# Attention's AV product with the exponentials as the stationary operand and a column of ones beside v

## The chip, the cores and the metric

The kernel runs on one core of one Trainium2 chip. The time is the device time of one execution in microseconds (us); the figure of a kernel is the median of its timed executions. Before the change it was 445.83 us (3 executions, 445.46 to 446.05). An execution counts as slow when it lies over 1.5% above the fastest of its kernel.

Engines: PE is TensorE (matmuls), "PEld" its weight loads, ACT is ScalarE, DVE is VectorE, POOL is GpSimd, SP is SyncE, which here only issues DMAs.

## The reference, cut to what matters

```python
# attention: q, k, v are [8 batches, 8 heads, 576, 64]; bias_table is [32, 8]
scores = q @ k.T / sqrt(64) + bias[bucket(|i - j|)]     # bias depends on the distance only
attn   = softmax(scores)                                # over the 576 keys
x      = (attn @ v), heads side by side                 # [4608, 512]
# "MoE" block (one expert)
h   = x @ w_in                                          # 512 -> 2048
g   = h + sin(alpha * h)**2 / (alpha + 1e-9)
out = g @ w_out                                         # 2048 -> 512, [4608, 512] fp32
```

The kernel computes exp(score/8) without subtracting the maximum, multiplies it by exp(bias) (a mask that differs from a constant only near the diagonal), forms the product with v and the sum over the keys, and divides.

## The kernel before: the parts that matter

One batch is 576 rows; there are 8 batches and four pairs of heads in each. Scores are kept transposed: keys on the partitions, queries on the free axis. `u` is the tile of exponentials of one pair, `[128 keys, 9 key blocks, 576 queries]`, where block 8 holds the last 64 keys of both heads.

A small scheduler in the kernel, run when the kernel is built, puts all work into a fixed order per engine, from estimated durations. Output matmuls (`mo`) are "fillers": they have no urgent reader, so the scheduler drops them into PE's waits during the attention of the next batch.

```python
def mm2(out, lhsT, rhs, start, stop):          # a 128-wide matmul as two of 64 stationary columns
    for z in range(2):
        nc.tensor.matmul(out=out[64*z : 64*z+64], lhsT=lhsT[:, 64*z : 64*z+64], rhs=rhs, ...)

# QK: one unit = one PSUM bank of scores = one exponential of 384 columns
for g in range(2):
    nc.tensor.matmul(out=sc.v[64*g : 64*g+64, ...], lhsT=kz[:, p, k0 : k0+64], rhs=qT[:, p, q0 : q0+n], ...)
nc.scalar.activation(out=u.v[:, k0 : k0+nc_, q0 : q0+n], in_=sc.v[...], func=AF.Exp, scale=0.125)

# AV: v is stationary, the exponentials stream through. y = 0: ones in place of v, so that the sums
# arrive on all 64 partitions of each head; y = 1: v itself. Columns streamed: 2 x 5 x n
for y in range(2):
    mm2(o[:, 0:n], vh if y else ones2, u.v[:, 8, q0 : q0+n], True, False)
    for c in range(4):
        for z in range(2):
            nc.tensor.matmul(out=o[64*z : 64*z+64, 0:n], lhsT=vs[..] if y else ones,
                             rhs=u.v[:, 4*z + c, q0 : q0+n], start=False, stop=(c == 3))
# 1/sum as exp(-ln(sum)) on ACT, then the product with it on DVE
nc.scalar.activation(out=ln.v[:, 0:n], in_=avs[0].v[:, 0:n], func=AF.Ln)
nc.scalar.activation(out=rd.v[:, 0:n], in_=ln.v[:, 0:n], func=AF.Exp, scale=-1.0)
nc.vector.tensor_tensor(out=xT[...], in0=avs[1].v[...], in1=rd.v[...], op=ALU.mult)

# ... cut: per batch, a table load, 16 sine units (PE sc -> ACT sine -> square -> DVE g), a table load
# ... cut: start-up: POOL reverses the mask table (m2, mh) that DMA brought in ascending order
```

The softmax here doesn't subtract the row's maximum and nothing guards it: scores larger than these inputs give would overflow.

Of the kernel before, what the change touches and what calls it, by code (L numbers as in the profile page):

```python
# [10 lines left out]
F16 = mybir.dt.float16  # L11
# [23 lines left out]
NBUF = {"sc": 4, "av": 2, "mo": 2, "u": 2, "g": 2, "s16": 3, "sq": 3, "outs": 2, "ln": 2, "rd": 2}  # L35


class Task:
    def __init__(self, engs, emit, deps, pri, nb=0.0):
        self.engs, self.emit, self.deps, self.pri, self.nb = engs, emit, list(deps), pri, nb  # L40
        self.allocs = []
        self.s_only = self.fill = self.tiled = False
        self.end = self.eng = None
# [11 lines left out]
class Plan:  # L55


    def __init__(self):
        self.tasks = []
        self.sin = self.in_qk = self.tiled = False  # L60
        self.used = self.share = 0
        self.warm = None
        self.rings = {k: [] for k in NBUF}

# [9 lines left out]
    def ready(self, t):  # L74
# [4 lines left out]
        for d in t.deps:  # L79
            if d.end is None:  # L80
                return None
            r = max(r, d.end - (LAT["PE"] if d.eng == "PE" and "PE" in t.engs else 0.0))
        for b in t.allocs:
            ring, n = self.rings[b.tag], NBUF[b.tag]
            if len(ring) >= n:
                for x in ring[-n].users:
                    if x.end is None:
                        return None
                    r = max(r, x.end)
        return r  # L90

    def run(self, t0):
        free = {e: t0 for e in ("PE", "ACT", "DVE", "POOL")}
        todo = list(self.tasks)
        while todo:
# [3 lines left out]
            for t in todo:  # L99
# [6 lines left out]
                for e in t.engs:  # L106
# [3 lines left out]
                    if e == "PE" and t.tiled != self.tiled:  # L110
                        st += D_MODE
# [29 lines left out]
            if e == "PE":  # L141
                self.tiled = t.tiled
# [9 lines left out]
            todo.remove(t)  # L152


WINDOW = 700
D_MODE = 0.0
WARM_END = 40.0
# [3 lines left out]
T_START = 5.4  # L161
T_M2 = 11.0
T_V0 = 13.0
T_TR1 = 34.0
T_W = 28.0
T_WO = 52.0
# [3 lines left out]
LN_PRI = -2000  # L170
# [17 lines left out]
def kernel(  # L188
# [49 lines left out]
    vs = [sgl.tile([128, 4, H, D], F16, name=f"v{i}") for i in range(2)]  # L238

    vhs = [sgl.tile([128, NP, 2, D], F16, name=f"vh{i}") for i in range(2)]  # L240
    ones = sgl.tile([128, D], F16, name="ones")
    ones2 = sgl.tile([128, 2, D], F16, name="ones2")
    m2 = sgl.tile([128, H, XW], F16, name="m2")
    mh = sgl.tile([128, NP, 192], F16, name="mh")
# [8 lines left out]
    m2r = wv[:, 2 * 5 * H * D : 2 * 5 * H * D + H * XW].rearrange("p (h x) -> p h x", h=H)  # L253
# [34 lines left out]
    def new_ln():  # L288
        return tp.tile([128, 384], F32, name="lnd", tag="lnd", bufs=NBUF["ln"])

    def new_rd():
        return tp.tile([128, 384], F32, name="rd", tag="rd", bufs=NBUF["rd"])

# [9 lines left out]
    def new_sc():  # L303
        return ps.tile([128, 512], F32, name="sc", tag="sc", bufs=NBUF["sc"])
# [14 lines left out]
    def load_kqT(t):  # L319
# [3 lines left out]
        nc.sync.dma_start(out=kz[64:128, :, S : 2 * S], in_=kraw[64:128, :, :])  # L323
        nc.sync.dma_start_transpose(out=qTs[t % 2][:, :, :], in_=staged_q.ap()[t])

    def load_v16(t):
        vp = v[t].rearrange("h s d -> s h d")
        for c in range(4):
            nc.gpsimd.dma_start(  # L329
                out=vs[t % 2][:, c], in_=vp[128 * c : 128 * c + 128],  # L330
            )
        vq = v[t].rearrange("(hp two) s d -> two s hp d", two=2)
        for z in range(2):
            nc.gpsimd.dma_start(
                out=vhs[t % 2][64 * z : 64 * z + 64, :, z, :], in_=vq[z, 512:S]
# [10 lines left out]
    def cast_v(eng, t):  # L346
        for c in range(4):
            eng.tensor_copy(out=vs[t][:, c], in_=vst[:, c])
        for z in range(2):
            eng.tensor_copy(  # L350
                out=vhs[t][64 * z : 64 * z + 64, :, z, :], in_=vhst[64 * z : 64 * z + 64]
# [18 lines left out]
    def clear_v(eng, i):  # L370
        eng.memset(vhs[i][0:64, :, 1, :], 0.0)
        eng.memset(vhs[i][64:128, :, 0, :], 0.0)

    def mm2(out, lhsT, rhs, start, stop):

        for z in range(2):
            nc.tensor.matmul(  # L377
                out=out[64 * z : 64 * z + 64], lhsT=lhsT[:, 64 * z : 64 * z + 64], rhs=rhs,
                start=start, stop=stop,
            )  # L380

    def warm(n):
        x = new_mo()
        for _ in range(n):
            mm2(x, zz[:, 0:128], zz, True, True)
# [6 lines left out]
    def load_m2r(h0, h1):  # L392

        nc.gpsimd.dma_start(
# [4 lines left out]
    def turn(p):  # L399
        nc.gpsimd.tensor_copy(  # L400
            out=m2[:, 2 * p : 2 * p + 2, :], in_=m2r[:, 2 * p : 2 * p + 2, ::-1]
        )

    load_nat(nat0[:, 0], 0, 2, k[0], nc.sync)
    nc.sync.dma_start(out=tabN, in_=bias_table)
    nc.sync.dma_start(out=phi_sb, in_=phi_h.ap())
    nc.sync.dma_start(out=id_sb, in_=idm.ap())
    load_nat(nat0[:, 1], 0, 2, q[0], nc.scalar)
# [4 lines left out]
    )  # L413
    nc.scalar.preload_act_table_set(EXP_SET)
    load_v32(0, nc.sync)
    for kq, src in ((0, k), (1, q)):
        load_nat(nat1[:, kq, 0:2], 2, 4, src[0], nc.gpsimd)

    nc.vector.memset(zz, 0.0)
    nc.vector.memset(kzs[0][0:64, :, S : 2 * S], 0.0)  # L420
    nc.vector.memset(kzs[0][64:128, :, 0:S], 0.0)
    clear_v(nc.vector, 0)
# [7 lines left out]
    nc.scalar.dma_start(out=e_dram.ap(), in_=e_sb)  # L430
    cast0(0, nc.vector)
    cast0(1, nc.gpsimd)
    nc.sync.dma_start(out=alphaN, in_=moe_alpha.rearrange("(f p) -> f p", p=128))
    nc.sync.dma_start(out=idf_sb, in_=idf.ap())
    nc.gpsimd.memset(ones, 1.0)
    nc.gpsimd.memset(ones2, 0.0)
    nc.gpsimd.memset(ones2[0:64, 0, :], 1.0)
    nc.gpsimd.memset(ones2[64:128, 1, :], 1.0)
    load_m2r(0, 2)
    for kq, src in ((0, k), (1, q)):  # L440
        load_nat(nat1[:, kq, 2:6], 4, H, src[0], nc.gpsimd)
    load_m2r(2, H)
    turn(0)
    cast_v(nc.gpsimd, 0)
    load_w_in16()
    for p in range(1, NP):
        turn(p)
    me = m2.rearrange("p (hp two) x -> p two hp x", two=2)
    nc.gpsimd.tensor_copy(out=mh[0:64, :, :], in_=me[0:64, 0, :, 0:192])
    nc.gpsimd.tensor_copy(out=mh[64:128, :, :], in_=me[64:128, 1, :, 64:256])  # L450
# [3 lines left out]
    clear_v(nc.gpsimd, 1)  # L454
    nc.gpsimd.memset(kzs[1][0:64, :, S : 2 * S], 0.0)
    nc.gpsimd.memset(kzs[1][64:128, :, 0:S], 0.0)
    cast_v(nc.gpsimd, 1)
# [14 lines left out]
    def plan_tr(t, p, kq, pri, nb, deps=()):  # L472
# [36 lines left out]
        return [plan.add(eng, cp, [m], pri, use=[b])]  # L509
# [18 lines left out]
    def plan_pair(t, p, kqt, first, gate, ub, band_nb):  # L528
# [3 lines left out]
        units, head = [], []  # L532
        for w in range(2):
            units += [(w, 4, 0)]
            for c in range(0, 4, 1 + w):
                units += [(w, c, 0), (w, c, 1)]
        if t == 0 and p == 0:
            units = [units[x] for x in (1, 3, 0, 2, 4)] + units[5:]
        for i, (w, c, z) in enumerate(units):
            q0, n = WIN[w]  # L540
            nc_ = 1 if w == 0 or c == 4 else 2
            b, sc = Buf("sc"), Cell()

            def qk(e, i=i, w=w, c=c, z=z, q0=q0, n=n, nc_=nc_, sc=sc):
# [8 lines left out]
                sc.v = new_sc()  # L553
                for y in range(nc_):
                    for g in range(2):
                        k0 = S * g + 512 if c == 4 else S * z + 128 * (c + y) + 64 * g
                        nc.tensor.matmul(  # L557
                            out=sc.v[64 * g : 64 * g + 64, n * y : n * y + n],
                            lhsT=kzs[t % 2][:, p, k0 : k0 + 64],
                            rhs=qTs[t % 2][:, p, q0 : q0 + n], start=True, stop=True,  # L560
                        )

            def ex(e, w=w, c=c, z=z, q0=q0, n=n, nc_=nc_, sc=sc):
                k0 = 8 if c == 4 else 4 * z + c
                nc.scalar.activation(  # L565
                    out=u.v[:, k0 : k0 + nc_, q0 : q0 + n], in_=sc.v[:, 0 : n * nc_],
                    func=AF.Exp, scale=0.125,
                )

            base = PB + 100 * (16 * p + i)  # L570
            m = plan.add({"PE": nc_ * t_pe(n)}, qk, kqt, base, after=head, new=[b] + ([ub] if i == 0 else []))
            head = head or [m]
            x = plan.add({"ACT": t_act(n * nc_)}, ex, [m] + gate, base + 20, use=[b, ub])
            if c == 4:
                if w == 0:
                    done[(w, 4, 0)] = done[(w, 4, 1)] = x
                    continue
# [5 lines left out]
                x = plan.add({"DVE": 0.17}, bh, [x] + mh_tasks, base + 10, nb=band_nb, use=[ub])  # L583
                done[(w, 4, 0)] = done[(w, 4, 1)] = x
                continue
            for y in range(nc_):
                done[(w, c + y, z)] = x
            if z == 0:
                continue
            for cc in range(c, c + nc_):  # L590
# [4 lines left out]
                def bd(e, cc=cc, lo=lo, hi=hi):  # L595
# [7 lines left out]
                x = plan.add({"DVE": 0.07 + (hi - lo) / 960.0}, bd,  # L603
                             [done[(w, cc, 0)], done[(w, cc, 1)]], base + 10, nb=band_nb,
                             use=[ub])
                done[(w, cc, 0)] = done[(w, cc, 1)] = x
        return u, done

    av_last = []
# [222 lines left out]
```

## Time and profile before

| reading | value | view |
|---|---|---|
| time | 445.83 us | timed executions |
| busy: PE / ACT / DVE | 95 / 86 / 59% of the span | page, part 1 |
| period of steady batches | 45.87 us | sine table loads in the timeline |
| exponential phase: PE, ACT busy | 28.74, 28.15 of 28.77 us | windows |
| sine phase: PE, ACT busy | 16.86, 15.87 of 16.86 us | windows |

Busy times and the chain, from the page (busy us, share of the span, x instructions; then the chain of work that ended last, by engine):

```profile
PE 423.1 (95%) x4934; PEld 306.1 (69%) x4934; DVE 262.4 (59%) x554; ACT 382.9 (86%) x834; POOL 84.5 (19%) x95
...
PE 71%; ACT 16%; issue 3%; DVE 3%; DMA 3%; POOL 2%; ACTq 0%; DVEq 0%; POOLq 0%
```

PE's 95% is no proof that PE is the limit: matmuls overlap and their ends are modelled. What tells is how far apart they start. L377 in these lines is line 377 of the kernel, the helper `mm2`.

The timeline of ACT shows one table load for the sine and one for the exponential per batch; here two sine loads four batches apart (start us, duration us, what):

```profile
189.24 1.28 ACT L756 ACT_TABLE_LOAD   x1
...
372.71 1.28 ACT L756 ACT_TABLE_LOAD   x1
```

(372.71 - 189.24) / 4 gives the period, 45.87 us. The windows view splits it (window, length, then busy us of each engine with its instructions, granted clock of PE, DMA share, GB/s). The first is a sine phase, the second an exponential phase, the third the same four batches:

```profile
core 0: us, PE busy (x) PEld busy (x) DVE busy (x) ACT busy (x) POOL busy (x), PEclk, DMA share, GB/s
97.59:114.45 16.86, 16.86 (x164) 11.12 (x160) 13.59 (x24) 15.87 (x25) 9.24 (x8) 1.00 1.75 180
114.45:143.22 28.77, 28.74 (x392) 22.55 (x389) 15.45 (x40) 28.15 (x74) 0.00 (x0) 1.00 0.30 44
189.24:372.71 183.47, 181.61 (x2188) 134.63 (x2185) 115.43 (x253) 178.90 (x397) 23.26 (x22) 1.00 0.60 72
```

ACT is busy 178.90 of 183.47 us, 97.5%.

The groups that the change touches (line, engine, operation, out<-in, shapes, count | busy us, mean ns of one | idle before them and who ended it):

```profile
L631 PE MATMUL av<-u,ones 128*64 128x384 f16 x256 | 27.6, 332 | 0.0
L647 ACT ACTIVATE lnd<-av 128x384 f32<-128x384 f32 x32 | 17.8, 556 | 1.9 <-PE av L631 1.0
L651 ACT ACTIVATE rd<-lnd 128x384 f32<-128x384 f32 x32 | 16.7, 523 | 1.0
L598 DVE TENSOR_TENSOR u<-u,m 128x512 f16<-128x512 f16 x64 | 28.3, 442 | 31.2 <-ACT u L565 27.9 <-POOL m L400 3.2
L631 PEld LDWEIGHTS <-v 128*64 128x64 f16 x512 | 30.7, 112 | 3.9
```

The waits between 10 and 50 us, the first batch (who waited <- for whom: us in total, times, longest):

```profile
DVE u L581 <- POOL mh L450: 6.6, 1, 6.6
...
PE sc L557 <- DVE qT L470: 5.3, 2, 4.6
```

### The profile page before, as it was taken

Reading aid. Unit: us, or ns where it says so; the run is one execution under the profiler, and the core shown is the slowest. Engines: PE = TensorE matmul, PEld = TensorE weight load, DVE = VectorE, ACT = ScalarE, POOL = GpSimd, SP = SyncE. Lnnn points to the kernel's source line nnn. Section 1 sums busy time; section 2 is a strip of 40 time slices with the busy share of each in tenths; the row PEclk is TensorE's granted clock in tenths of the full one; section 3 lists DMA queues with packets and bytes.
Section 4 is the critical chain, followed back from the end, with each engine's and each line's share of the span. In section 5 each row is a group of like instructions: output and inputs, shape, how many; then the busy total and the mean of one; then the engine's idle time right before and its main releaser. Section 6 shows DMA issues by size and latency. Waiting matters only on the chain.

```text
span 444.2 us, 12031 instructions
## 1 busy us (share of the span) xinstructions
PE 423.1 (95%) x4934; PEld 306.1 (69%) x4934; DVE 262.4 (59%) x554; ACT 382.9 (86%) x834; POOL 84.5 (19%) x95
## 2 busy tenths in 40 slices
PE   5579999999999999999999999999999999999996
PEld 3356657876688668865886688657876787666663
DVE  4447695549654865576456755685568545927400
ACT  3459999999999999999999999999999999946511
POOL 3792931016000700080008000400000000000000
PEclk8659999999999999999999999999999999999999
DMA  9999999939900996199209960980000000011111
GB/s 193 181 206 144 163 163 147 194 81 181 110 25 26 106 146 143 42 147 168 39 27 98 156 140 1 160 104 25 27 26 0 27 26 25 2 49 47 49 72 71
DMA packets 136118, 41.51 MB, mean 93 GB/s; under 512 B 122520, under 2 KB 130768, under 8 KB 136064
## 3 DMA queue, kind: packets, MB, share of 16 engines
q0 software_dynamic: 89392, 17.67, 47.3%
q1 hardware_dynamic: 46400, 22.79, 23.4%
q8 instruction: 38, 0.62, 0.6%
q10 hardware_dynamic: 272, 0.30, 0.2%
q14 instruction: 16, 0.13, 0.1%
HBM read 37.56 MB, written 16.52 MB: 122 GB/s over the span
## 4 chain that ended last, share of the span: by engine, by line
PE 71%; ACT 16%; issue 3%; DVE 3%; DMA 3%; POOL 2%; ACTq 0%; DVEq 0%; POOLq 0%
PE mo L377 24%; PE sc L377 18%; PE sc L557 14%; PE av L631 12%; ACT s L694 6%; ACT u L565 4%; PE av L377 3%; ACT L756 2%; ACT sq L701 2%; DVE g L708 1%; DMA w_out<-e_dram 1%; DMA tabL<-in_bias_table_dram 1%; DVE kz L470 1%; ACT rd L651 1%; ACT lnd L647 1%
## 5 line engine op out<-in xcount | busy, mean ns | idle before, releaser
L565 ACT ACTIVATE u<-sc 128x384 f16<-128x384 f32 x448 | 175.3, 527 | 7.6 <-PE sc L557 7.4
L377 PE MATMUL mo<-w_out,g 128*64 128x512 f16 x1152 | 172.2, 379 | 0.0
L557 PE MATMUL sc<-qT,kz 128*64 128x192 f16 (+1 forms) x1152 | 134.8, 296 | 8.8 <-DVE qT L470 5.3
L377 PE MATMUL sc<-xT,w_in 128*64 128x512 f16 x1152 | 132.7, 379 | 1.3 <-DVE g L708 1.3
L598 DVE TENSOR_TENSOR u<-u,m 128x512 f16<-128x512 f16 (+1 forms) x192 | 73.5, 400 | 72.1 <-ACT u L565 68.6
L557 PEld LDWEIGHTS <-kz 128*64 128x64 f16 x1152 | 84.7, 112 | 42.8 <-issue 10.6
L708 DVE SCALAR_TENSOR_TENSOR g<-sq,inv_a,sc 128x512 f16<-128x512 f16 x144 | 102.0, 745 | 20.6 <-PE mo L377 10.7
L377 PEld LDWEIGHTS <-w_in 128*64 128x64 f16 x1152 | 80.3, 110 | 44.1 <-issue 2.8
L694 ACT ACTIVATE s<-sc,alphaT 128x512 f16<-128x512 f32 x144 | 92.5, 678 | 3.5 <-PE sc L377 2.5
L377 PEld LDWEIGHTS <-g 128*64 128x64 f16 x1152 | 79.1, 110 | 22.5
L329 POOL DMA_DIRECT2D v<-in_v_dram x24 | 22.3, 1065 | 176.3 <-PE av L631 176.3
L701 ACT ACTIVATE sq<-s 128x512 f16<-128x512 f16 x75 | 47.2, 629 | 2.3
L662 DVE TENSOR_TENSOR xT<-av,rd 128x384 f16<-128x384 f32 (+1 forms) x68 | 29.4, 437 | 32.9 <-ACT rd L651 24.8
L631 PE MATMUL av<-u,ones 128*64 128x192 f16 (+1 forms) x512 | 44.8, 291 | 0.0
L631 PE MATMUL av<-u,v 128*64 128x192 f16 (+1 forms) x512 | 44.7, 291 | 0.0
L703 DVE TENSOR_TENSOR sq<-s 128x512 f16<-128x512 f16 x69 | 28.9, 420 | 11.4 <-ACT s L694 11.1
L647 ACT ACTIVATE lnd<-av 128x384 f32<-128x384 f32 x64 | 28.9, 451 | 7.3 <-PE av L631 6.5
L468 ACT ACTIVATE outs<-mo 128x512 f32<-128x512 f32 x15 | 8.9, 595 | 29.3 <-PE mo L377 29.3
L631 PEld LDWEIGHTS <-ones 128*64 128x64 f16 x512 | 30.8, 112 | 5.0
L631 PEld LDWEIGHTS <-v 128*64 128x64 f16 x512 | 30.7, 112 | 3.9
L651 ACT ACTIVATE rd<-lnd 128x384 f32<-128x384 f32 x64 | 28.7, 449 | 1.4
L377 PE MATMUL av<-u,ones 128*64 128x192 f16 (+1 forms) x128 | 20.5, 291 | 2.7 <-DVE u L581 2.7
(59 smaller groups left out, 194.0 us busy)
## 6 DMA issues: line engine op xcount, KB each, us to landing
out_dram<-outs SPq DMA_DIRECT2D x36, 256.0 KB, 2.0
staged_k<-in_k_dram POOLq DMA_DIRECT2D x6, 576.0 KB, 13.6
staged_q<-in_q_dram POOLq DMA_DIRECT2D x6, 576.0 KB, 16.7
kz<-kraw SPq DMA_DIRECT2D x12, 288.0 KB, 6.3
v<-in_v_dram POOLq DMA_DIRECT2D x24, 128.0 KB, 5.4
w_out<-in_v_dram SPq DMA_DIRECT2D x8, 256.0 KB, 5.4
w_in<-in_moe_w_in_dram POOLq DMA_DIRECT2D x4, 512.0 KB, 8.8
w_out<-in_moe_w_out_dram POOLq DMA_DIRECT2D x4, 512.0 KB, 8.8
```

The lines of the kernel that those rows point to most:

```text
L377: nc.tensor.matmul(out=out[64 * z : 64 * z + 64], lhsT=lhsT[:, 64 * z : 64 * z + 64], rhs=rhs, start=start, stop=stop,)
L557: nc.tensor.matmul(out=sc.v[64 * g : 64 * g + 64, n * y : n * y + n], lhsT=kzs[t % 2][:, p, k0 : k0 + 64], rhs=qTs[t % 2][:, p, q0 : q0 + ...
L565: nc.scalar.activation(out=u.v[:, k0 : k0 + nc_, q0 : q0 + n], in_=sc.v[:, 0 : n * nc_], func=AF.Exp, scale=0.125,)
L598: nc.vector.tensor_tensor(out=io, in0=io, in1=m2[:, 2 * p : 2 * p + 2, x0 : x0 + hi - lo], op=ALU.mult,)
L631: nc.tensor.matmul(out=o[64 * z : 64 * z + 64, 0:n], lhsT=vs[t % 2][:, c, 2 * p + z, :] if y else ones, rhs=u.v[:, 4 * z + c, q0 : q0 + n] ...
L647: nc.scalar.activation(out=ln.v[:, 0:n], in_=avs[0].v[:, 0:n], func=AF.Ln)
L651: nc.scalar.activation(out=rd.v[:, 0:n], in_=ln.v[:, 0:n], func=AF.Exp, scale=-1.0)
L662: nc.vector.tensor_tensor(out=xT[:, p, (x0 + a) % XN : (x0 + a) % XN + m - a], in0=avs[1].v[:, a:m], in1=rd.v[:, a:m], op=ALU.mult,)
L694: nc.scalar.activation(out=s16.v, in_=h.v, func=AF.Sin, scale=alphaT[:, f : f + 1])
L701: nc.scalar.activation(out=sq.v, in_=s16.v, func=AF.Square)
L703: k_of(e).tensor_tensor(out=sq.v, in0=s16.v, in1=s16.v, op=ALU.mult)
L708: nc.vector.scalar_tensor_tensor(out=gcell[b].v[:, f, :], in0=sq.v, scalar=inv_a[:, f : f + 1], in1=h.v, op0=ALU.mult, op1=ALU.add,)
```

## The change

Its intent: stream fewer columns through PE and take work off ACT.

1. **AV turned round.** 128 queries' exponentials are stationary, and v streams with a column of ones beside it (65 columns per head). The sum then lands next to the product as one column per query, so 1/sum is a tiny DVE reciprocal. The result has queries on the partitions and is transposed back by PE.
2. **Two-bank QK units.** One exponential covers 768 columns in two PSUM banks. The MoE product keeps one-bank units, so the PSUM ring becomes two pools that change size between the phases.
3. **Full width.** Every matmul of the steady batches uses 128 stationary columns at once instead of two column tiles of 64.
4. **Start-up.** The mask table is stored as DMA brings it and read backwards by DVE, so POOL no longer reverses it; the start-up's loads are reordered and the scheduler's constants retuned.

```diff
-    def mm2(out, lhsT, rhs, start, stop):
-        for z in range(2):
-            nc.tensor.matmul(out=out[64 * z : 64 * z + 64], lhsT=lhsT[:, 64 * z : 64 * z + 64], ...)
+    def full(out, lhsT, rhs, start, stop):
+        nc.tensor.matmul(out=out, lhsT=lhsT, rhs=rhs, start=start, stop=stop)

+    m2 = m2r[:, :, ::-1]            # the mask read backwards; POOL's reversals are gone

+        # QK unit: both banks, one exponential
+        sc.v = new_sc(2)
+        full(sc.v[:, z, 0:384], kz[:, p, k0 : k0 + 128], qT[:, p, q0 : q0 + n], True, True)   # z = 0, 1
+        nc.scalar.activation(out=uz[:, :, c, 0:384], in_=sc.v[:, :, 0:384], func=AF.Exp, scale=0.125)

-        # AV: ones or v stationary, u streaming; ln and exp on ACT   (as shown above)
+        # AV: per 128 queries qc; VC = 65
+        full(av.v[:, x0 : x0 + 2 * VC], u.v[:, 8, qc : qc + 128], vhs[t % 2][:, p, :], True, False)
+        for z in range(2):
+            for c in range(4):
+                full(av.v[:, x0 + VC * z : x0 + VC * z + VC],
+                     u.v[:, 4 * z + c, qc : qc + 128], vs[t % 2][:, c, 2 * p + z, :], False, ...)
+        nc.vector.reciprocal(out=r, in_=a[:, :, :, D])
+        nc.vector.tensor_tensor(out=xn..., in0=a[:, :, :, 0:D], in1=r (broadcast), op=ALU.mult)
+        nc.tensor.transpose(out=tr.v[...], in_=xn.v[:, i], identity=id_sb)
+        copy_on(e, xT[...], tr.v[...])                      # DVE or ACT

-T_TR1 = 34.0      # us from which batch 1's k and q may be transposed
+T_TR1 = 30.0
 # ... cut: pools, ones columns, start-up order, other constants
```

## The prediction

> **What bounds the kernel now.** The table loads in the timeline give a steady period per batch of 45.9 us (from 189.2 to 372.7 us, four batches), split by the windows view into an exponential phase of 28.8 us (PE busy 28.7, ACT 28.1, DVE 15.2) and a sine phase of 16.9 us (PE 16.9, ACT 15.9, DVE 13.6). Granted clock 1.00. The busy share of PE is no proof, so I sum streams by spacing: a pair of 64-column matmuls takes 0.215 us at 512 columns, 0.163 at 384, 0.082 at 192. Per batch: QK 8.8, AV 9.8 (half of it the ones matmuls that broadcast the sums), the two MoE products 27.6; sum 46.2. So PE streams without gaps, with ACT right behind. The first batch is different: its exponential phase ends only at 50.0 us; the granted clock is 0.5 to 0.7 between 10 and 30 us, and the waits name POOL: DVE waits 6.6 us for the reversed table mh, PE 4.6 us behind a qT copy.
>
> **What changes.**
> - PE: AV becomes, per 128 queries, 8 matmuls of 65 columns and one of 130, plus one 128-column transpose. Spacing fits about 2 + 0.416 ns per column (96 columns 42, 512 columns 215). Estimate from it: 8 x 29 + 56 = 0.29 us; 20 such per batch 5.8, transposes 1.1, so 6.9 against 9.8. This holds only if a full-width weight load every 29 ns is possible. The start-up's six warm 96-column transposes run at 42 ns each behind full 128-column loads (95 to 98 ns each, against 110 for a 64-column load), so such a load costs at most 42 ns. The Trainium skill ("TensorE: Matmul & The Clock Gate", weight-path perf modes) gives Fast Weight Load to loads of 128 non-fp32 columns, and "TensorEngine Tiling (Array Packing)", restrictions, denies it to column tiling; the shorter load agrees. At 42 ns per load AV would still take 8.9. I take 7.4: 2.4 us less per batch.
> - QK and MoE stream the same columns; halving their instructions gains nothing, they were already stream bound.
> - ACT: the logarithm and its exponential go (57.7 us busy in all), exponentials go from 13 plus one instructions per pair to 7 longer ones; some copies of xT come. About 8 us less per batch: ACT leaves the critical path of the exponential phase, the sine phase stays as it is.
> - DVE: reciprocal, multiply and copy replace one multiply: about 5 us more per batch. Masks are read backwards; I assume that they keep their rate.
> - POOL: the four reversals and the two mh copies go; the first batch's masks come earlier.
>
> **On the critical path.** In the steady state only PE counts: 7 batches x 2.4 = 17 us. In the first batch the mh wait and ACT's chain of about 1.6 us per pair count, and there is no filler on PE: about 7 us. New waits (two-bank units refilled only after a long exponential; transposes waiting for DVE) give back perhaps 1.
>
> **Prediction: 422 us, 80% range 413 to 434. Faster by over 2%: 0.93; within 2%: 0.06; slower: 0.01.**
>
> **Signs.** Right: period near 43.5 us; AV groups of nine at 0.29 to 0.33 us; mo and sc at 0.215 us per 512 columns; exponential phase near 26 us with ACT visibly idle, sine phase near 17; first sine table before 44 us; mask operations at the same mean times. Wrong: AV matmuls spaced 40 ns or more; PE idle before the transposes or before two-bank QK units; sine phase longer.
>
> **What would make it wrong.** Weight loads slower than the 65-column stream; reversed masks at half rate, which would put DVE near its limit; the first batch bound by DMA rather than by POOL; a period held by ACT or DVE in the sine phase.

## The result, and the profile after

The changed kernel takes 424.4 us (4 executions, 423.51 to 425.71; the kernel before beside it 445.64). The ratio is 0.9526, 95% interval 0.9504 to 0.9548. A ratio is the mean time of one kernel's fast runs over that of the other's of the same rounds, so it is not quite the ratio of the medians.

| reading | before | after |
|---|---|---|
| period of steady batches | 45.87 us | 43.80 us |
| output matmuls (full-width count) done in one such period, of 64 made | 56 | 64 |
| AV and its transposes on PE, per batch | 9.85 us | 7.10 us |
| first sine table load | 50.04 us | 46.51 us |
| second sine table load | 97.59 us | 99.02 us |
| end, after the last sine table load | 71.5 us | 61.3 us |

The AV row sums the distances from each AV matmul's start to the next start in the trace, over four steady batches.

From the page:

```profile
PE 400.9 (95%) x3518; PEld 232.2 (55%) x3518; DVE 293.2 (69%) x683; ACT 337.2 (80%) x502; POOL 77.9 (18%) x88
...
PE 87%; DMA 7%; SPq 2%; DVE 2%; POOL 1%; issue 0%; ACT 0%; ACTq 0%; POOLq 0%
```

ACT has gone from the chain (16% to 0%), and DMA's share has grown from 3 to 7%. The sine loads four batches apart, and the windows (an exponential phase, a sine phase, the four batches):

```profile
187.44 1.28 ACT L775 ACT_TABLE_LOAD   x1
...
362.65 1.28 ACT L775 ACT_TABLE_LOAD   x1
```

```profile
161.65:187.44 25.79, 25.79 (x302) 17.40 (x300) 16.82 (x48) 22.55 (x32) 0.00 (x0) 1.00 0.63 80
187.44:205.43 17.99, 17.99 (x104) 8.65 (x102) 15.57 (x29) 16.53 (x27) 9.24 (x8) 1.00 1.51 148
187.44:362.65 175.21, 175.21 (x1603) 104.18 (x1601) 129.62 (x310) 156.43 (x231) 23.27 (x22) 1.00 0.66 80
```

ACT is now busy 156.43 of 175.21 us (89%). The groups:

```profile
L402 PE MATMUL av<-v,u 128*128 128x65 f16 x1280 | 56.1, 195 | 0.0
L593 ACT ACTIVATE u<-sc 128x768 f16<-128x768 f32 x192 | 148.6, 811 | 27.1 <-PE sc L402 22.0 <-ACT u L593 2.3
L621 DVE TENSOR_TENSOR u<-u,m2r 128x512 f16<-128x512 f16 x64 | 27.1, 424 | 4.4 <-ACT u L593 2.3
L663 DVE RECIPROCAL rd<-av 128x6 f32<-128x6 f32 x32 | 6.2, 194 | 28.7 <-PE av L402 28.6
L664 DVE TENSOR_TENSOR xn<-av,rd 128x384 f16<-128x384 f32 x32 | 17.8, 557 | 1.1
L402 PEld LDWEIGHTS <-u 128*128 128x128 f16 x1440 | 56.6, 99 | 9.7 <-ACT u L593 2.4
```

The masks read backwards take 424 ns where they took 442, so they kept their rate; the Trainium skill ("VectorE: DVE Perf Modes", the 2x_1P mode) allows a step of plus or minus 1 in it, and the trace agrees. PE's timeline shows three AV groups in a row, each one matmul of 130 columns and eight of 65 (a group spans its nine matmuls; durations overlap, 195 ns on average for a matmul every 29 ns, so read the starts):

```profile
210.48 0.23 PE L402 MATMUL av<-vh,u 128*128 128x130 f16 x1
210.55 0.41 PE L402 MATMUL av<-v,u 128*128 128x65 f16 x8
210.80 0.22 PE L402 MATMUL av<-vh,u 128*128 128x130 f16 x1
210.85 0.41 PE L402 MATMUL av<-v,u 128*128 128x65 f16 x8
211.10 0.22 PE L402 MATMUL av<-vh,u 128*128 128x130 f16 x1
```

From 210.48 to 210.80 to 211.10: 0.30 to 0.32 us per group, 29 ns (median) per 65-column matmul with a full weight load before each.

Two things in the table do not fit a gain of a bit over 2 us in each of 8 batches. The first two batches took longer than before, 99.02 us against 97.59; and the tail shrank by 10 us, although the MoE products that make it up were not made shorter. The second is bookkeeping: the kernel before got only 56 of each batch's 64 output matmuls into its period and ran 183 of its 576 after the last table load; the changed kernel ran 133. **A period says nothing without the number of fillers in it.** The first is a real loss. The first sine table load came 3.5 us sooner (46.51 against 50.04), and the stretch from it to the second took 5.0 us longer (52.5 against 47.6). PE's timeline shows where:

```profile
35.92 0.49 PE L402 MATMUL sc<-qT,kz 128*128 128x384 f16 x2
39.32 0.69 PE L500 MATMUL mo<-id_sb,nat 96*64 96x96 f16 x12 [2.91 <-DMA nat<-in_k_dram]
39.95 0.39 PE L674 MATMUL av<-id_sb,xn 128*128 128x128 f16 x2
40.13 0.69 PE L402 MATMUL sc<-qT,kt 128*128 128x288 f16 x2
43.50 0.69 PE L500 MATMUL mo<-id_sb,nat 96*64 96x96 f16 x12 [2.69 <-DMA nat<-in_q_dram]
44.12 1.46 PE L402 MATMUL sc<-qT,kz 128*128 128x192 f16 x8
...
53.80 0.69 PE L500 MATMUL mo<-id_sb,nat 96*64 96x96 f16 x12 [2.82 <-DVE qT L483]
```

The transposes of batch 1's k and q (L500) stand in PE's order ahead of the last QK units of batch 0, and their loads are late. A third wait, for DVE's copy of qT, ends at 53.8 us. The granted clock drops too: 0.50 in the window from 40 to 45 us and 0.54 from 55 to 60 us. The Trainium skill ("TensorE: Matmul & The Clock Gate", the HAM clock gate) says that an array that was idle for one window of about 3.4 us gets half its clock. The trace agrees only roughly: the clock was halved with PE idle for 2.7 to 2.9 us at a time, while waits of 2.8 and 2.4 us that ended at 10.0 and 13.6 us did not halve it.

### The profile page after: what moved, and what is told of

Its sections match the earlier page's. It is cut to its first block, busy times and chain, and to the rows that moved or that the text cites. A ratio compares the mean times of both kernels' runs of the same rounds, so it can differ in the third digit from the quotient of the medians.

```text
span 423.9 us, 8745 instructions
## 1 busy us (share of the span) xinstructions
PE 400.9 (95%) x3518; PEld 232.2 (55%) x3518; DVE 293.2 (69%) x683; ACT 337.2 (80%) x502; POOL 77.9 (18%) x88
## 4 chain that ended last, share of the span: by engine, by line
PE 87%; DMA 7%; SPq 2%; DVE 2%; POOL 1%; issue 0%; ACT 0%; ACTq 0%; POOLq 0%
PE sc L402 45%; PE mo L402 29%; PE av L402 10%; DMA nat<-in_q_dram 5%; PE av L674 2%; SPq L360 1%; DMA w_out<-in_v_dram 1%; DVE kt L529 1%; DMA natx<-in_k_dram 1%; SPq L363 1%; POOL w_in L381 1%; PE mo L500 0%; DVE xn L664 0%; POOL nat L376 0%; DVE outs L483 0%
## 5 line engine op out<-in xcount | busy, mean ns | idle before, releaser
L593 ACT ACTIVATE u<-sc 128x768 f16<-128x768 f32 (+1 forms) x224 | 166.2, 789 | 27.2 <-PE sc L402 22.0
L402 PE MATMUL mo<-w_out,g 128*128 128x512 f16 x576 | 156.7, 379 | 0.0
L402 PE MATMUL sc<-xT,w_in 128*128 128x512 f16 x576 | 133.4, 384 | 0.0
L402 PE MATMUL sc<-qT,kz 128*128 128x192 f16 (+1 forms) x512 | 90.8, 292 | 3.4 <-ACT qT L481 2.4
L402 PEld LDWEIGHTS <-w_in 128*128 128x128 f16 x576 | 56.3, 99 | 66.5 <-issue 3.3
L621 DVE TENSOR_TENSOR u<-u,m2r 128x512 f16<-128x512 f16 (+1 forms) x192 | 70.5, 388 | 17.0 <-ACT u L593 14.5
L402 PEld LDWEIGHTS <-g 128*128 128x128 f16 x576 | 55.9, 98 | 45.5
L402 PEld LDWEIGHTS <-u 128*128 128x128 f16 x1440 | 56.6, 99 | 9.7 <-ACT u L593 2.4
L402 PEld LDWEIGHTS <-kz 128*128 128x128 f16 x512 | 43.7, 99 | 23.3 <-issue 4.1
L402 PE MATMUL av<-v,u 128*128 128x65 f16 x1280 | 56.1, 195 | 0.0
```

The source lines that it names most:

```text
L402: nc.tensor.matmul(out=out, lhsT=lhsT, rhs=rhs, start=start, stop=stop)
L593: nc.scalar.activation(out=o, in_=x, func=AF.Exp, scale=0.125)
L621: nc.vector.tensor_tensor(out=io, in0=io, in1=m2[:, 2 * p : 2 * p + 2, x0 : x0 + hi - lo], op=ALU.mult,)
```

## The experiments

Theory: the gain is PE's shorter AV stream, which could only become time because ACT, equally full, was relieved as well; the first two batches gained nothing because loads for batch 1 came late in a fixed order. Rivals: PE's stream alone, or ACT's relief alone, made the gain; the full-width weight load is what makes the new AV pay; the start-up is bound by bytes. Ratios are to the kernel before, beside which each was run; that of the changed kernel is 0.9526.

### PE or ACT: relieving each of them in the kernel before

**b_few_ones**: four of the five steps of the ones matmuls dropped (wrong result).

```diff
-                for c in range(4):
+                for c in range(4 if y else 0):
```

> The kernel before, with only the first of the five steps of the ones matmuls left (wrong result on purpose: sums over the last 64 keys alone). PE's stream falls by about 3.9 us per batch, 31 in all; ACT's work is the same. If PE alone bound the kernel before: about 415 us. If ACT held the period (28.1 us busy of 28.8 in the exponential phase) and PE only filled it with output matmuls: the period stays near 45.7 us, the backlog of output matmuls left for the end goes (55 of them, 0.215 us each), and the whole is 430 to 437 us.

Measured: 432.54 us, ratio 0.9674. PE lost about 31 us of stream (worked out from the spacing: 3.9 us in each of 8 batches), and the kernel gained 14. The period over four batches, (370.36 - 187.41) / 4 = 45.74 us, is the same as before, now with all 64 fillers in it:

```profile
187.41:370.36 182.95, 175.15 (x1988) 119.29 (x1985) 116.82 (x256) 174.47 (x397) 22.93 (x22) 1.00 0.60 76
```

The waits of PE in that stretch:

```profile
PE sc L377 <- DVE g L708: 7.7, 4, 1.9
```

PE is visibly idle, 7.8 of 182.95 us, and waits for the sine phase's chain through ACT and DVE. So PE's stream did not hold the period. That ACT held it follows only together with b_neither below: ACT is busy 174.47 of 182.95 us here (95%), and the engines' orders are fixed by the scheduler, which may itself hold a period.

**b_no_ln**: the logarithm and its exponential dropped, a constant multiplied in (wrong result).

```diff
-            l_ = plan.add({"ACT": t_act(n)}, lg, prev, base + LN_PRI, new=[lb], use=[bs[0]])
-            r = plan.add({"ACT": t_act(n) + 0.04}, rc, [l_], base + LN_PRI, new=[rb], use=[lb])
+            r = prev[0]
-                        in0=avs[1].v[:, a:m], in1=rd.v[:, a:m], op=ALU.mult,
+                        in0=avs[1].v[:, a:m], in1=rdc[:, a:m], op=ALU.mult,
```

> The kernel before without the logarithm and the exponential of it; the multiply takes a constant instead (wrong result on purpose); the ones matmuls still run. ACT loses 57.7 us of busy time, PE's stream is the same. If PE's total stream counts (46.2 us per batch with all its output matmuls): 438 to 446 us, with a shorter exponential phase paid back by fewer fillers in it. If ACT alone held the kernel before: 425 us or less.

Measured: 440.60 us, ratio 0.9854. ACT lost 57.7 us, and the kernel gained 6. The steady period fell to 43.4 us at first, but with 48 fillers in it; 205 were left for after the last table load. PE's total stream did not change, and most of what the period lost came back at the end.

**b_neither**: both edits.

> The two edits of the last two runs together (wrong result on purpose): PE 31 us less, ACT 57.7 us less. If both engines were at their limit and each relief alone is held by the other: 405 to 415 us, more than the sum of the two single gains. If the gains simply add, the sum of what the two single runs gained.

Measured: 418.60 us, ratio 0.9368, 28 us gained. That is above the range, but the single gains sum to 14 + 6 = 20, so the two reliefs do need each other. Over four steady batches:

```profile
173.58:340.25 166.67, 165.62 (x1924) 122.06 (x1922) 114.88 (x255) 156.92 (x333) 23.25 (x22) 1.00 0.68 80
```

The period is 166.67 / 4 = 41.67 us with 56 fillers in it, against 45.74 with 64 in b_few_ones. The 8 missing fillers are worth 1.7 us of PE (8 x 0.2155); even if all of that came off the period, over 2 us are left, and only the edit on ACT can have taken those. So ACT's logarithm and exponential held that period. Whether by their busy time or by their place in the chain from the sums to the product, these two runs do not tell.

### Giving ACT its load back in the changed kernel

**act_ballast**: two useless exponentials on ACT after each AV group.

```diff
+        for o in (idle1, idle2):
+            plan.add({"ACT": t_act(n) + 0.04}, ballast(o), prev, base + NORM_PRI)   # AF.Exp of zeros
```

> The changed kernel with two useless exponentials of 384 or 192 columns on ACT after each AV group, about what the logarithm and its exponential took before (57.7 us busy in all). PE streams exactly the same columns. If PE's stream alone counted: 423 to 426 us. If relief of ACT was needed as well (ACT has 39.1 us busy of 43.8 in a period, and about 7 come back): the period rises to 45.5 to 46.5 us and the whole to 435 to 443 us.

Measured: 453.79 us, ratio 1.0190: slower than the kernel before, and outside what either theory expected. The timeline shows why the run does not settle the question: some exponentials fell into the sine phase, and each time two more table loads were put in.

```profile
198.68 0.69 ACT L723 ACTIVATE s<-sc,alphaT 128x512 f16<-128x512 f32 x1
199.39 1.28 ACT L673 ACT_TABLE_LOAD   x1
200.68 0.62 ACT L673 ACTIVATE idle<-zz 128x192 f32<-128x192 f16 x2
201.32 1.28 ACT L723 ACT_TABLE_LOAD   x1
```

**act_copy**: the same with copies, which need no table.

```diff
-                nc.scalar.activation(out=o[:, 0:n], in_=zz[:, 0:n], func=AF.Exp)
+                nc.scalar.activation(out=o[:, 0:n], in_=zz[:, 0:n], func=AF.Copy)
```

> The run act_ballast again with the two useless operations as copies instead of exponentials, because the exponentials called for two more table loads per batch (2.6 us of ACT) that the kernel before does not have. ACT has 39.1 us busy of 43.8 in a period of the changed kernel; the copies should bring about 6. If relief of ACT was needed for the gain: period of steady batches 44.5 to 46 us and the whole 429 to 438 us. If PE's stream alone counted: 423 to 427 us.

Measured: 429.39 us, ratio 0.9633, at the low end of what was expected of the theory. The ballast was smaller than estimated: ACT's busy time went from 337.2 to 370.4 us, 33 us, where the logarithm and its exponential had been 57.7. Over four steady batches ACT was busy 172.63 of 176.88 us, 97.6%, as in the kernel before, and the period had begun to grow, from 43.80 to 44.22 us. So about 4 us of ACT work per batch uses up the room that the change made, and here it is busy time alone that counts, since nothing waits for the copies. The remaining part of the old load was not tried in this form.

### The two-bank QK units alone

**one_bank**: QK units and exponentials back to one bank; AV stays new.

```diff
-                sc.v = new_sc(2)
+                sc.v = new_sc(1)                      # one head's bank; units doubled
-                    o, x = uz[:, :, c, 0:384], sc.v[:, :, 0:384]
+                    o, x = uz[:, z, c, 0:384], sc.v[:, 0:384]
```

> The changed kernel with its QK units taken back to one bank each: 14 exponentials of 384 or 288 columns per pair instead of 7 of 768 or 576, and PSUM as a ring of single banks throughout. AV stays as changed. Theory (PE's stream sets the period; ACT has 4.7 us of slack in 43.8): the period grows by less than 0.3 us, 422 to 428 us in all. Rival (the two-bank units are a needed part of the gain): period 45 us or more, 433 us or more.

Measured: 427.24 us, ratio 0.9573: 0.5% slower than the changed kernel (0.9573 / 0.9526). The expected time held, the expected sign of the period did not: it fell to 42.9 us with 56 fillers in it, and the fillers ran at the end (184 after the last table load). ACT was busy 161.88 of 171.62 us. The two-bank units and the changing pools are worth half a per cent; the rest of the gain does not need them.

### Why AV pays on PE: the weight load or the array's mode

**av_halves**: only the AV matmuls split in two column tiles of 64.

```diff
-                full(av.v[:, x0 : x0 + 2 * VC], u.v[:, 8, qc : qc + 128], vhs[t % 2][:, p, :], True, False)
+                for g in range(2):
+                    r, k0 = slice(64 * g, 64 * g + 64), qc + 64 * g
+                    full(av.v[r, x0 : x0 + 2 * VC], u.v[:, 8, k0 : k0 + 64], vhs[t % 2][:, p, :], True, False)
     # ... the eight 65-column matmuls likewise; the scheduler's cost of a group 0.31 -> 0.45
```

> The changed kernel with each AV matmul split in two with 64 stationary columns (column tiles side by side), the same number of streamed columns per tile. Right result. Theory (AV pays because a full 128-column weight load fits under a 65-column stream of 29 ns): two half loads do not fit; from 22 ns per 64-column load in the kernel before, 44 ns per pair, an AV group of nine takes 0.42 us or more instead of 0.30, the period is 46 us or more and the whole 440 us or more. Rival (the two half loads run side by side under the stream as well): 424 to 428 us.

Measured: 434.45 us, ratio 0.9737, between the two. My theory of the weight load was wrong, as PE's timeline shows:

```profile
211.80 0.38 PE L402 MATMUL mo<-w_out,g 128*128 128x512 f16 x1
212.11 0.25 PE L402 MATMUL av<-vh,u 128*64 128x130 f16 x2
212.19 0.42 PE L402 MATMUL av<-v,u 128*64 128x65 f16 x16
212.44 0.22 PE L402 MATMUL av<-vh,u 128*64 128x130 f16 x2
212.50 0.42 PE L402 MATMUL av<-v,u 128*64 128x65 f16 x16
```

From 212.11 to 212.44: 0.33 us for a group of nine pairs, where the full-width group took 0.30 to 0.32. Two half loads nearly fit under the stream as well. But from the 512-column matmul to the first AV matmul it is 309 ns on average, against 216 in the changed kernel, and from the last AV matmul to the next QK matmul 128 ns against 31. So a change between full width and column tiles costs 93 to 97 ns each way. Eight entries and eight exits per batch make 1.5 of the 1.8 us by which the period grew (45.6 against 43.8). The Trainium skill ("TensorEngine Tiling (Array Packing)", key properties) says that changing the tiling mode drains the array. The trace agrees that each change costs time, 93 to 97 ns; that the drain is what takes it is the skill's reading, not shown here.

**all_halves**: every matmul and transpose in column tiles of 64, so that the mode never changes.

```diff
     def full(out, lhsT, rhs, start, stop):
-        nc.tensor.matmul(out=out, lhsT=lhsT, rhs=rhs, start=start, stop=stop)
+        for z in range(2):
+            r = slice(64 * z, 64 * z + 64)
+            nc.tensor.matmul(out=out[r], lhsT=lhsT[:, r], rhs=rhs, start=start, stop=stop)
     # ... the transposes of xn likewise
```

> The changed kernel with every full-width matmul and transpose (QK, AV, both MoE products) split into two of 64 stationary columns, so that PE never changes between full width and column tiles. In av_halves a pair of half AV matmuls took about 31 to 36 ns inside a group against 30 for a full one, but each entry into the group and each exit from it took 93 to 97 ns more; 8 groups per batch make 1.5 of the 1.8 us by which its period grew. Theory (the switch costs, not the narrower weight load): the entries and exits vanish, the steady period is 43.7 to 44.3 us and the whole 424 to 429 us. Rival (full-width weight loads are what makes the new AV pay): the period is 45 us or more and the whole 433 us or more.

Measured: 429.86 us, ratio 0.9624. The steady period is 176.61 / 4 = 44.15 us, as the theory of the mode expected: in column tiles throughout, a batch costs 0.35 us more than at full width, not 1.8 (AV and its transposes take 7.41 us of PE against 7.10). This run also keeps most of the gain, 3.8 of 4.7%, so full width is not what the change mainly lives on. The whole is 1% slower than the changed kernel and just above the expected range; the difference beyond the steady batches lies in batches 1 to 3 (53.5, 46.0 and 44.7 us against 52.5, 44.6 and 43.8), and its cause stays open.

### The start-up

**tr_late**: one constant.

```diff
-T_TR1 = 30.0
+T_TR1 = 46.0
```

> The changed kernel with one number altered: the scheduler may place the transposes of batch 1's k and q only from 46 us on instead of 30 us. In the trace of the changed kernel PE stood 2.9 and 2.7 us for those loads at 39 and 43 us, with four QK units of the first batch behind them in PE's order, and the granted clock fell to 0.5. Theory (a fixed order on PE put work whose data was late ahead of work that was ready): these two waits go, the first sine table is loaded near 41 us instead of 46.5, and the whole is about 418 us (414 to 421). Rival (the start-up is bound by DMA bytes, so some other load is then waited for): 423 to 426.

Measured: 420.11 us (5 fast runs, 416.16 to 422.16; a sixth, 423.68, was slow), ratio 0.9389, so 1.4% faster than the changed kernel: in the theory's range, at its slow end, with a wide spread. The two waits are gone and the first sine table is loaded at 39.7 us. But the transposes' copies now fall on DVE in batch 0's sine phase, and PE waits 3.7 us for DVE's g there, so part of the gain is given back.

**nat_first**: batch 1's k and q loaded before w_in.

```diff
+    for kq, src in ((0, k), (1, q)):
+        load_nat(nat2[:, kq], 0, H, src[1], nc.gpsimd)
     load_w_in16()
-    for kq, src in ((0, k), (1, q)):
-        load_nat(nat2[:, kq], 0, H, src[1], nc.gpsimd)
```

> The changed kernel with the loads of batch 1's k and q issued on the POOL queue before w_in instead of after it; nothing else. Theory (late k and q hold PE): the two waits go, 417 to 422 us. Rival (DMA is full until 40 us, so w_in becomes late by what k and q gained, and the first MoE product waits instead): 423 to 427.

Measured: 421.66 us, ratio 0.9449. The waits for k and q are gone, w_in is not waited for, and the first sine table is loaded at 38.5 us, 8 us sooner. Yet the second batch then takes 55.7 us, because of a new wait (waits of DVE, then of PE, from 70 to 95 us):

```profile
DVE outs L483 <- DMA out_dram<-outs: 6.3, 1, 6.3
```

```profile
PE av L674 <- DVE xn L664: 6.0, 1, 6.0
```

SP issues the output stores in order behind the transposing loads of batch 2's k and q. Both output buffers were full, DVE could not copy a third output, and DVE's next work, the one that PE waited for, stood behind that copy.

**nat_outs**: nat_first with four output buffers.

```diff
-NBUF = {... "outs": 2, "xn": 3}
+NBUF = {... "outs": 4, "xn": 3}
```

> The run nat_first with four output buffers in place of two. In its trace the output copy on DVE stood 6.3 us at 81 us because both buffers were held by stores queued on SP behind the transposing loads of batch 2, and PE stood 6.0 us behind DVE. Theory: two more buffers take that wait away, about 415.5 us (413 to 418). Rival (the stores stay queued and the wait only moves to a later copy): 420 to 423 us.

Measured: 414.38 us (5 fast runs, 412.38 to 418.38; a sixth, 418.90, was slow), ratio 0.9303, as expected. The second sine table is loaded at 85.7 us instead of 99.0. This version is correct and beats both kernels, the changed one by 2.3% (0.9303 / 0.9526).

**nat_outs_m2r**: and the first mask load issued from SP instead of ACT.

```diff
-    load_m2r(nc.scalar, 0, 2)
+    load_m2r(nc.sync, 0, 2)
```

> The run nat_outs with the first load of the reversed table issued from SP instead of ACT. In the trace of the changed kernel ACT's queue stood 5.6 us on that load's dependence and the copy of qT behind it, so the first QK unit came 2.4 us late. Theory: a further 1 to 2 us, about 414 us. Rival (the first masks become late by as much, since SP's queue is behind its own loads): the same as nat_outs within 1 us.

Measured: 414.54 us, ratio 0.9294, interval 0.9274 to 0.9314. It cannot be told from nat_outs (0.9266 to 0.9340), so the rival's reading, no more than 1 us, is what was seen.

Not run: the new AV alone in the kernel before, and the mask read backwards or the retuned constants alone. What each of these is worth by itself stays open.

## Why the prediction was right or wrong

The time, 424.4 us, lies near the predicted 422, and the direction was right: AV's shorter stream on PE, with ACT relieved, is what paid. That the number came so close is partly luck. The first two batches gave nothing where 7 us were expected, and the rest of the kernel gave 21.7 us where 17 were.

- **AV's stream: right, and undersized.** "I take 7.4: 2.4 us less per batch." The trace gives 7.10 against 9.85, 2.75 less; the spacing rule predicted 6.9 before I added a margin for the weight load, and no margin was needed. Groups took 0.30 us, as foreseen.
- **The reason given for it: half right.** A full-width load does fit under 29 ns. But it is not what the gain hangs on: half loads nearly fit too (av_halves, all_halves). What full width everywhere spares is the change of mode at 93 to 97 ns that a mix would pay (the kernel before, in column tiles throughout its steady batches, did not pay it either); the prediction did not mention it.
- **"So PE streams without gaps, with ACT right behind": wrong.** My sum of 46.2 us was more than the period of 45.87, and I let that pass. Only 56 of 64 output matmuls were in the period; with the other 8 (7.75 x 0.2155 us) taken off, PE's stream is about 44.5 us, so some 1.3 us per batch were gaps, and ACT held the period. b_few_ones and b_neither show it: 31 us less on PE left the period at 45.7, and taking ACT's two operations away as well brought it to 41.7.
- **"In the steady state only PE counts": right for the kernel after, not before.** It came out in the sum because fillers that miss the period are paid at the end. b_no_ln gained 6 us and b_few_ones 14, both 28: the change paid because it relieved both engines. With ACT at 89%, the gaps shrank to about 0.3 us per batch (43.8 less the streams' sum of 8.8 + 7.1 + 27.6 = 43.5). I had predicted that new waits would give back 1 us in all; in the steady batches there were fewer waits instead.
- **The step that failed: "In the first batch the mh wait and ACT's chain ... count, ...: about 7 us."** Half of it came, 3.5 us by the first sine table load, and the second batch lost it again. At the second sine table load the changed kernel was 1.4 us later than the one before with 7 more output matmuls done (1.5 us): the first two batches gained nothing, although AV alone should have brought 2 x 2.75. The mh wait did go. In its place came waits for batch 1's k and q (2.9 and 2.7 us) and for DVE's copy of qT (2.8 us), and a halved clock. The prediction had named "the first batch bound by DMA rather than by POOL" as a risk; tr_late, nat_first and nat_outs show that it was order and buffers, not bytes: the same bytes in another order, and two more buffers, bring the second sine table 13 us forward.
- **Steady side.** From the second sine table to the end the gain is 346.6 - 324.9 = 21.7 us: 6 x 2.75 = 16.5 from AV, 1.5 from the 7 output matmuls done earlier, and the rest, about 4, is what is left over; the gaps that closed, about 1 us per batch by the sums above, would account for it, but were not measured apart.
- **ACT: 8 us less per batch was too much.** Busy time fell by (382.9 - 337.2) / 8 = 5.7 us, in part because 23 copies of xT (about 10 us in all) moved to ACT. DVE: about 5 us more per batch predicted, (293.2 - 262.4) / 8 = 3.9 measured. Neither shows in the time: ACT kept some 4 us of room per batch (act_copy).
- **Signs.** Period near 43.5: 43.8. Exponential phase near 26: 25.8. Sine phase near 17: 18.0, so the sign "sine phase longer" came up, though with PE full throughout and 15 fillers in it where the phase shown of the kernel before had 12. AV groups, 0.30 us on average, and mask operations, 424 against 442 ns: right. First sine table before 44 us: 46.5, wrong.

## What to carry to other kernels

Where a scheduler fills waits with deferrable work, compare the amount of filler per period before believing a period: two engines can both look full, and relief of one then comes back as work at the end. A sum of streams that exceeds the period is a warning, not a rounding. In a fixed order, look for work whose data comes late standing ahead of work that is ready; the order of loads and a pair of buffers were worth a further 2.3% here.

## What the Trainium skill lacked or had wrong

- "TensorEngine Tiling (Array Packing)", key properties: that changing the mode drains the array is stated, its cost is not. Here it was 93 to 97 ns on each entry and exit (309 against 216 ns, 128 against 31 ns).
- "TensorE: Matmul & The Clock Gate", back-to-back issue gap: it gives about 81 ns per matmul for a sustained stream of weight loads and matmuls of 128 columns and about 131 ns for 512, and keeps its formula of N / 2.4 + 2.5 ns for an isolated matmul. Here, with a weight load before each, the 128-column transposes ran at 56 ns and the 512-column matmuls at 216 ns; 65 columns ran at 29 ns. So the formula (56, 216 and 30 ns) fits the stream, and the sustained figures do not.
- "TensorE: Matmul & The Clock Gate", LDWEIGHTS: the time is said to grow with the number of columns, P / 1.2, which would be an estimated 53 ns for 64 columns and 107 ns for 128. Here a 64-column load in a column tile took 112 ns and a full 128-column load 99 ns (Fast Weight Load, which the prediction cites, would make the full load the faster one, but gives no 112 ns for half of one), and neither set the pace: loads were hidden down to 29 ns per matmul at full width, and to about 33 ns per pair in column tiles.
